# S4 and squared-ReLU gated mix, forward and gradients: an inverse FFT on half the frequencies, with mirrored frequencies in one PSUM tile and evacuations of two banks

## The chip, the cores and the metric

The kernel runs on one core of a Trainium2 chip. A core has engines that run side by side, each through its own queue in order: TensorE (PE in the profile; its weight loads are PEld), VectorE (DVE), ScalarE (ACT), GpSimd (POOL) and SyncE (SP). SP and ACT also issue the DMAs of this kernel. The metric is the time of one execution in device microseconds (us), as the median of several runs.

## The reference

The kernel computes a gated mix of two branches and all its gradients, in bfloat16, with sequence length L = 2048, width D = 448, N = 256 complex states per channel and a hidden width of F = 1792:

```python
g = sigmoid((x * gate_w).sum(-1, keepdims=True))
P = exp(dt*A * l);  K = einsum("dn,dnl,dn->dl", C, P, dt*B).real   # A, B, C complex
y = irfft(rfft(pad(u)) * rfft(pad(K)))[:L]                         # length 4096
a = y + u * Dskip
b = relu(x @ w1 + b1)**2 @ w2 + b2
out = g * a + (1 - g) * b
```

The outputs are `out` and 14 gradients (of u, the real and imaginary parts of A, B and C, log_dt, Dskip, w1, b1, w2, b2 and the gate). The gradient of the convolution needs two more transforms of the same kind: with dA the gradient that reaches the branch a, the gradient of K is the correlation of dA with u, and the gradient of u is the correlation of dA with K. So there are three forward transforms (u, dA, K) and three inverse ones (dK, y, du).

## The kernel before

**The transform.** A sequence of 2048, zero-padded to 4096, is transformed in two matrix steps over 64 × 64, with a round trip through HBM (a DRAM scratch buffer) between the two, since the second step needs the other index on the partitions. All 448 channels go side by side in the free dimension, so every matmul has 448 columns of data. The four steps are methods of `FFTCtx`:

- `fwd1` (L121–139) loads the sequence (tile `xs`), multiplies it with the constant `F1BD`, evacuates PSUM tiles `ps` to staging tiles `st` (name `st_g` here) and writes these to the scratch buffer `gd` or `gd2`.
- `fwd2` (L141–157) loads that buffer in one DMA as `s1`, multiplies with `M2` in tiles of 32 output rows, four of them side by side in the 128 PSUM partitions, and evacuates to a spectrum tile `[P, 16, 2, D]` (16 frequencies per partition group, real and imaginary part).
- `inv1` (L165–181) takes a spectrum, multiplies it with `MI`, evacuates to staging tiles (name `st_h`) and writes `hd` or `hd2` in 16 DMAs.
- `inv2` (L183–199) loads that back in 16 DMAs as tiles `hs`, multiplies with `Etw` in tiles of 32 output rows, and evacuates to a result tile (`dk_tl` or `res_tl`), which `tl_store` writes in four DMAs (L119).

The input is real, so frequency 63 − k1 of the first index holds the conjugate of frequency k1. The kernel before uses that in the forward step only (`kk = k1 if k1 < 32 else 63 - k1`): `fwd2` computes all 64 values of k1 from 32, and the inverse sums over all 64.

Each evacuation takes one bank of PSUM, 448 values per partition. `evac` (L97–103) gives two of three to ACT (L100) and the third to DVE (L102); `dma` (L93–95) alternates between the queues of SP and ACT. The PSUM pools `psF` and `psF2` hold four such tiles, the staging pools `fstg` and `fstg2` hold two of each kind, so a third staging tile waits until the DMA of the first has ended. The constants are loaded from HBM in fp32 and cast on DVE (L77–90), twice: once for each of the two places where transforms stand.

**The order of the work.** The program is one line of stages:

1. Gate and dA, parameter preparation (up to 81 us in the trace).
2. First transforms (L683–701, 81 to 284 us): `fwd1` of u and dA, `fwd2` of both (spectra `SP_U`, `SP_DA`, also stored to `sp_d`), their product `Pc` (`cmul_spec`, L586–600, on DVE), the inverse of it to `dk_tl`, and the store to `dk_d`.
3. The table stage (L706–729, to 1174 us): 17 chunks. For each, `multipliers` (L312–364) computes powers on DVE and ACT (L335 to L363), `doubling` (L366–377) builds the tables `XW` and `Yt` on DVE (L375 `U`, L376 `V`, L377 the sum), `kgen` (L398–420) makes a part of K on PE from them, and `run_chunk` (L486–571) contracts them with dK for the parameter gradients. `load_dk` (L482) brings `dk_d` back as `DK`, in two DMAs of 64 partitions each. The tables of a chunk are emitted with high priority, one chunk ahead of the contraction.
4. Transforms again (L734–842, 1174 to 1464 us): `fwd1` of K, parameter gradients (L746–827, on DVE, results `ob_…` stored by L822), `fwd2` of K (`SP_K`), then for y and du the stored spectrum is loaded (`SPx`, L833) and multiplied with `SP_K` on DVE (`PcY`, `PcU`), then `inv1` of both, `inv2` of both, and the stores to `y_d` and `du_d`.
5. The dense branch (from L844: `Un` loaded by L848, weights `w1h`, `w2h` by L894 and L896) and the final sums (L1004–1075), to 1937 us.

The order within each engine's queue is not written out by hand. The Tile framework takes the instructions in program order with their priorities and buffers and schedules them; each engine then runs its queue in order. A changed number of instructions or buffers in one stage can therefore change where instructions of the next stage stand.

Of the kernel before, what the change touches and what calls it, by code (L numbers as in the profile page):

```python
# [14 lines left out]
fp32 = mybir.dt.float32  # L15
# [4 lines left out]
P = 128  # L20
# [3 lines left out]
def host_consts():  # L24
    c = {}
    F1 = np.zeros((128, 2, 128), np.float64)
    j1 = np.arange(32)[:, None]
    k1 = np.arange(32)[None, :]
    ph = 2 * np.pi * j1 * (k1 + 0.5) / 64
    for g in range(4):  # L30
        hh, g2 = g // 2, g % 2
        F1[g * 32:(g + 1) * 32, hh, g2 * 64 + 0:g2 * 64 + 32] = np.cos(ph)
        F1[g * 32:(g + 1) * 32, hh, g2 * 64 + 32:g2 * 64 + 64] = -np.sin(ph)
    c["F1BD"] = F1.reshape(128, 256)
    M2 = np.zeros((128, 64, 2, 32), np.float64)
    j0 = np.arange(64)[:, None]
    k0 = np.arange(32)[None, :]
    for k1v in range(64):
        T = np.exp(-2j * np.pi * (j0 * (k1v + 0.5) / 4096 + j0 * k0 / 64))
        s = 1.0 if k1v < 32 else -1.0  # L40
        M2[0::2, k1v, 0, :] = T.real
        M2[1::2, k1v, 0, :] = -s * T.imag
        M2[0::2, k1v, 1, :] = T.imag
        M2[1::2, k1v, 1, :] = s * T.real
    c["M2"] = M2.reshape(128, 64 * 2 * 32)
    MI = np.zeros((128, 2, 4, 128), np.float64)
    k0 = np.arange(32)[:, None]
    l0 = np.arange(64)[None, :]
    E = np.exp(2j * np.pi * k0 * l0 / 64)
    for g in range(4):  # L50
        MI[g * 32:(g + 1) * 32, 0, g, 0:64] = E.real
        MI[g * 32:(g + 1) * 32, 0, g, 64:128] = E.imag
        MI[g * 32:(g + 1) * 32, 1, g, 0:64] = -E.imag
        MI[g * 32:(g + 1) * 32, 1, g, 64:128] = E.real
    c["MI"] = MI.reshape(128, 2 * 4 * 128)
    Et = np.zeros((128, 64, 32), np.float64)
    k1 = np.arange(64)[:, None, None]
    l0 = np.arange(64)[None, :, None]
    l1 = np.arange(32)[None, None, :]
    l = 64 * l1 + l0  # L60
    C = (2.0 / 4096) * np.exp(2j * np.pi * (k1 + 0.5) * l / 4096)
    Et[0::2] = C.real
    Et[1::2] = -C.imag
    c["Etw"] = Et.reshape(128, 64 * 32)
    return {k: v.astype(np.float32) for k, v in c.items()}


class FFTCtx:
# [52 lines left out]
    def fwd1(self, src_dram2d, gd, pool, tag="xs"):  # L121
# [19 lines left out]
    def fwd2(self, gd, sp_out, pool, tag="s1"):  # L141
        nc = self.nc
        c = self.c
# [3 lines left out]
        M2 = c["M2"]  # L147
        for k1l in range(16):
            for ro in range(2):
                ps = self.psum.tile([P, 512], fp32, tag="ps", name="ps")  # L150
                for k1g in range(4):
                    k1 = 16 * k1g + k1l
                    kk = k1 if k1 < 32 else 63 - k1
                    col = (k1 * 2 + ro) * 32
                    nc.tensor.matmul(ps[32 * k1g:32 * k1g + 32, 0:D], lhsT=M2[:, col:col + 32], rhs=s1[:, kk, :],
                                     start=True, stop=True, tile_position=(0, 32 * k1g))
                self.evac(sp_out[:, k1l, ro, :], ps[:, 0:D])

# [5 lines left out]

    def inv1(self, pspec, hd):  # L165
        nc = self.nc
        MI = self.c["MI"]
        for k1g in range(4):
            for q in range(4):
                st = self.stg.tile([P, 4, D], bf16, tag="st", name="st_h")  # L170
                for jj in range(4):
                    k1l = q * 4 + jj
                    ps = self.psum.tile([P, 512], fp32, tag="ps", name="ps")
                    for ri in range(2):
                        col = (ri * 4 + k1g) * 128
                        nc.tensor.matmul(ps[:, 0:D], lhsT=MI[:, col:col + 128], rhs=pspec(k1l, ri), start=(ri == 0), stop=(ri == 1))  # L176
                    self.evac(st[:, jj, :], ps[:, 0:D])
                k1base = 16 * k1g + q * 4
                dst = bass.AP(tensor=hd, offset=k1base * 128 * D,
                              ap=[[D, 128], [128 * D, 4], [1, D]])  # L180
                self.dma().dma_start(dst, st[:])

    def inv2(self, hd, dst_tl, ipool, tag="hs"):  # L183
        nc = self.nc
        Et = self.c["Etw"]
        for q in range(4):
            hs = ipool.tile([P, 4, 4, D], bf16, tag=tag, name=tag)
            for jj in range(4):
                src = bass.AP(tensor=hd, offset=(q * 4 + jj) * D,
                              ap=[[64 * D, 128], [16 * D, 4], [1, D]])  # L190
                self.dma().dma_start(hs[:, jj], src)
            for jj in range(4):
                l0l = q * 4 + jj
                ps = self.psum.tile([P, 512], fp32, tag="ps", name="ps")
                for l0g in range(4):
                    l0 = 16 * l0g + l0l
                    nc.tensor.matmul(ps[32 * l0g:32 * l0g + 32, 0:D], lhsT=Et[:, l0 * 32:(l0 + 1) * 32], rhs=hs[:, jj, l0g, :],
                                     start=True, stop=True, tile_position=(0, 32 * l0g))
                self.evac(dst_tl[:, l0l, :], ps[:, 0:D])

    def inv(self, pspec, hd, dst_tl):
        self.iv_i = getattr(self, "iv_i", 0) + 1
        self.inv1(pspec, hd)
        with self.tc.tile_pool(name=f"fftiv{self.iv_i}", bufs=2) as ipool:
            self.inv2(hd, dst_tl, ipool)
# [398 lines left out]
def kernel(ctx, tc, A_u, A_A_re, A_A_im, A_B_re, A_B_im, A_C_re, A_C_im, A_log_dt, A_Dskip,  # L604
# [80 lines left out]
    with tc.tile_pool(name="spB0", bufs=1) as spB0:  # L685
# [12 lines left out]
        with tc.tile_pool(name="spB1", bufs=1) as spB1:  # L698
            dk_tl = spB1.tile([P, 16, D], bf16, name="dk_tl")
            fft.inv(lambda k1l, ri: Pc[:, k1l, ri, :], hd, dk_tl)  # L700
            fft.tl_store(dk_d.ap(), dk_tl)
# [40 lines left out]
    with tc.tile_pool(name="spk", bufs=1) as spk:  # L742
# [363 lines left out]
```

## Time and profile before

| | |
|---|---|
| time, median of 3 runs | 1941.33 us (1940.83, 1941.33, 1948.38) |
| span of the profiled execution | 1936.9 us, 22440 instructions |
| busy: PE, PEld | 993.5 us (51%), 545.7 us (28%) |
| busy: DVE, ACT, POOL | 1115.7 us (58%), 974.2 us (50%), 24.3 us |
| read from HBM, written to HBM | 78.39 MB, 59.64 MB |
| mean granted TensorE clock | 0.737 |

The profiled execution has no other time of its own than its span, 1936.9 us; the median of the runs is 4.4 us above it. In the profile's rows, "L100 ACT CAST st_h<-ps" is an instruction of line 100 on ACT that writes the tile `st_h` from `ps`; an arrow with an engine or "DMA" behind an idle time names what ended the wait. A page of the profile shows the span in 40 slices of 48 us each, with one digit a slice for each engine. Rows of one stretch of time give its length, then the busy time and the number of instructions of PE, PEld, DVE, ACT and POOL, the granted clock, the DMA engines' busy share, and GB/s.

### The profile page before, as it was taken

The numbers are of one execution on the slowest core, as the hardware profiler recorded it, in microseconds if no ns is written. First come the engines' busy times: TensorE is split into PE (matmuls) and PEld (weight loads), VectorE is DVE, ScalarE is ACT, GpSimd is POOL, SyncE is SP. The second block draws the span as 40 slices with busy tenths as digits, with TensorE's granted clock in tenths as the row PEclk, the third lists the DMA queues.
The fourth block names the chain that finished last, engine by engine and source line by source line (L and its number), as shares of the span: only waits on it lengthen the run. The fifth ranks groups of instructions, "written<-read, shape, count | busy, mean of one in ns | idle before, by whom it ended". The sixth has DMA issues, their size and how long they took to land. (4 is left out here: it accounts for less than half of the span.)

```text
span 1936.9 us, 22440 instructions
## 1 busy us (share of the span) xinstructions
PE 993.5 (51%) x8145; PEld 545.7 (28%) x8160; DVE 1115.7 (58%) x1983; ACT 974.2 (50%) x1588; POOL 24.3 (1%) x77
## 2 busy tenths in 40 slices
PE   0344513345444543454445554322644999999941
PEld 0111202233223322333223331101312545544520
DVE  3426359876677777777676523687222355076347
ACT  0134348757666766677666552511432645524314
POOL 0000000000000000000000000000000000000000
PEclk9957856567667666776677765655966999999975
DMA  6575572144443234323443466532786100000032
GB/s 158 154 217 231 191 232 39 39 79 80 79 79 71 53 75 79 74 54 70 79 79 77 81 112 183 187 139 70 247 286 203 34 18 13 6 1 18 17 114 76
DMA packets 245221, 198.23 MB, mean 102 GB/s; under 512 B 25395, under 2 KB 241334, under 8 KB 242934
## 3 DMA queue, kind: packets, MB, share of 16 engines
q1 hardware_dynamic: 128566, 97.70, 20.0%
q10 hardware_dynamic: 116544, 99.10, 18.9%
q8 instruction: 64, 1.05, 0.2%
q14 instruction: 47, 0.39, 0.1%
HBM read 78.39 MB, written 59.64 MB: 71 GB/s over the span
## 5 line engine op out<-in xcount | busy, mean ns | idle before, releaser
L561 PE MATMUL psA<-Q,csb_SELA 128*128 128x256 bf16 x448 | 110.7, 324 | 191.0 <-DVE Q L557 189.4
L550 PE MATMUL psz<-yts,DKZ 128*128 128x256 bf16 x448 | 109.5, 344 | 177.4 <-ACT yts L545 143.3
L557 DVE TENSOR_TENSOR Q<-zb,XT 128x512 bf16<-128x512 bf16 x224 | 94.0, 421 | 147.0 <-ACT zb L556 88.8
L556 ACT CAST zb<-psz 128x512 bf16<-128x512 f32 x224 | 125.5, 591 | 76.5 <-PE psz L550 18.9
L506 ACT ACTIVATE DKZ<-DK,cs_MASK 128x448 bf16<-128x448 bf16 x128 | 133.7, 1104 | 7.4 <-DMA DK<-dk_d 6.6
L543 PE MATMUL ytp<-identb,Yt 128*128 128x128 bf16 x896 | 95.5, 260 | 72.1 <-ACT XTp L521 70.8
L545 ACT COPY yts<-ytp 128x1024 bf16<-128x1024 bf16 (+1 forms) x128 | 113.9, 915 | 17.2 <-issue 7.2
L563 PE MATMUL psB<-Qs,csb_SELB 128*128 128x256 bf16 x448 | 111.5, 327 | 14.7 <-DVE Qs L558 14.2
L550 PEld LDWEIGHTS <-DKZ 128*128 128x128 bf16 x448 | 52.3, 119 | 206.2 <-issue 190.8
L100 ACT CAST st_h<-ps 128x448 bf16<-128x448 f32 x127 | 61.1, 537 | 97.1 <-DMA hd<-st_h 59.7
L543 PEld LDWEIGHTS <-Yt 128*128 128x128 bf16 x896 | 78.7, 119 | 85.7 <-issue 73.4
L558 DVE TENSOR_TENSOR Qs<-zb,XTsw 128x512 bf16<-128x512 bf16 x224 | 93.4, 420 | 7.1 <-DMA XTsw<-XTp 3.8
L176 PEld LDWEIGHTS <-cb_MI 128*128 128x128 bf16 x384 | 40.9, 108 | 178.3 <-issue 130.2
L563 PEld LDWEIGHTS <-csb_SELB 128*128 128x128 bf16 x448 | 44.0, 113 | 159.6 <-issue 143.4
L102 DVE CAST st_h<-ps 128x448 bf16<-128x448 f32 x65 | 39.3, 622 | 82.3 <-DMA hd<-st_h 57.0
L375 DVE TENSOR_TENSOR U<-XW,PRX 128x224 bf16<-128x224 bf16 (+4 forms) x80 | 71.6, 895 | 19.9 <-ACT XW L391 14.8
L176 PE MATMUL ps<-PcY,cb_MI 128*128 128x448 bf16 x128 | 39.1, 455 | 82.3 <-DVE st_h L102 41.8
L519 PE MATMUL xtp<-identb,XW 128*64 128x128 bf16 x896 | 63.7, 254 | 29.6 <-DVE XW L377 28.2
L375 DVE TENSOR_TENSOR U<-Yt,PRY 128x112 bf16<-128x112 bf16 (+2 forms) x96 | 74.1, 771 | 2.4 <-POOL Yt L385 1.9
L377 DVE TENSOR_TENSOR Yt<-U,V 128x112 bf16<-128x112 bf16 (+2 forms) x96 | 74.3, 774 | 0.8
L376 DVE TENSOR_TENSOR V<-Yt,PIY 128x112 bf16<-128x112 bf16 (+2 forms) x96 | 74.0, 770 | 0.0
L377 DVE TENSOR_TENSOR XW<-U,V 128x224 bf16<-128x224 bf16 (+4 forms) x80 | 71.7, 897 | 3.1
(259 smaller groups left out, 2201.5 us busy)
## 6 DMA issues: line engine op xcount, KB each, us to landing
XT<-XTp SPq DMA_DIRECT2D x64, 224.0 KB
XTsw<-XTp ACTq DMA_DIRECT2D x128, 112.0 KB
XTsw<-XTp SPq DMA_DIRECT2D x128, 112.0 KB
XT<-XTp ACTq DMA_DIRECT2D x64, 224.0 KB
hd<-st_h ACTq DMA_DIRECT2D x24, 448.0 KB
hd<-st_h SPq DMA_DIRECT2D x24, 448.0 KB
hs<-hd ACTq DMA_DIRECT2D x24, 448.0 KB
hs<-hd SPq DMA_DIRECT2D x24, 448.0 KB
```

The costliest lines, as they stand in the source:

```text
L176: nc.tensor.matmul(ps[:, 0:D], lhsT=MI[:, col:col + 128], rhs=pspec(k1l, ri), start=(ri == 0), stop=(ri == 1))
L375: nc.vector.tensor_tensor(out=U, in0=lo, in1=PR[:, lev].unsqueeze(2).to_broadcast([P, W, n, 2]), op=ALU.mult)
L377: nc.vector.tensor_tensor(out=tab[:, :, n:2 * n, :], in0=U, in1=V, op=ALU.add)
L506: nc.scalar.activation(dst, dkv, ACT.Copy, scale=cst["MASK"][:, 2 * s + tt:2 * s + tt + 1])
L543: nc.tensor.transpose(ytp[:, qq, h * P:(h + 1) * P], src, T.identb[:])
L545: nc.scalar.copy(yts[:, 0:nq, :], ytp[:, 0:nq, :])
L550: nc.tensor.matmul(psz[:, qq, :], lhsT=DKZ[:, q0 + j].rearrange("p s a t -> p (s a t)"), rhs=yts[:, j, :], start=True, stop=True)
L556: nc.scalar.copy(zb[:], psz[:])
L557: nc.vector.tensor_tensor(out=Q[:], in0=zb[:], in1=XT[:, l0:l0 + 2, :], op=ALU.mult)
L558: nc.vector.tensor_tensor(out=Qs[:], in0=zb[:], in1=XTsw[:, l0:l0 + 2, :], op=ALU.mult)
L561: nc.tensor.matmul(psA[:], lhsT=cst["SELA"][:, 110 - 2 * dc:238 - 2 * dc], rhs=Q[:, qq, :], start=(dc == 0), stop=(dc == CC - 1))
L563: nc.tensor.matmul(psB[:], lhsT=cst["SELB"][:, 110 - 2 * dc:238 - 2 * dc], rhs=Qs[:, qq, :], start=(dc == 0), stop=(dc == CC - 1))
```

## The change

The inverse now sums only over the 32 values of k1 that are not conjugates of another, and takes twice the real part by its constants. `M2`, `MI` and `Etw` are laid out anew for that (`M2` keeps its size, `MI` shrinks from 1024 to 256 columns, `Etw` from 2048 to 1024). What this does to each step:

- `fwd2`: a PSUM tile of two banks, real and imaginary part, holds two values of kk, each with kk and its mirror 63 − kk in 64 of the 128 partitions. A matmul has 64 output rows instead of 32; there are 64 of them instead of 128, and 16 evacuations of 896 values instead of 32 of 448. The spectrum tile keeps its shape, with another meaning of its index.
- `inv1`: matmuls over 64 rows, two row tiles of the array side by side (`tile_position=(64*kk2, 0)`), 64 instead of 128; 16 evacuations of 896 values; 8 DMAs to `hd` of 448 KB instead of 16.
- `inv2`: 8 DMAs of 448 KB from `hd` instead of 16, each now to 64 partitions with runs of 2 × 448 values (before: to 128 partitions with runs of 448 values); 64 matmuls over 64 rows with 32 output rows each; 8 evacuations of 896 values instead of 16 of 448.
- `fwd1`: the same matmuls and DMAs, with evacuations of 896 values, 16 instead of 32.

All PSUM tiles of the transforms are now `[P, 2, 512]` in fp32, with the pools still at four: eight banks instead of four. The rest of the kernel is untouched; its lines stand 9 further down from `S4Tables` on (L477 is the old L468), and `evac` is L112 and L114, the write of `hd` L190, its load L199.

```diff
 # host_consts: M2, MI and Etw laid out anew, for kk = 0..31 with its mirror 63 - kk
-    M2 = np.zeros((128, 64, 2, 32), np.float64)
+    M2 = np.zeros((128, 32, 2, 2, 32), np.float64)
-    MI = np.zeros((128, 2, 4, 128), np.float64)
+    MI = np.zeros((2, 2, 32, 2, 2, 64), np.float64)
-    Et = np.zeros((128, 64, 32), np.float64)
+    Et = np.zeros((2, 32, 2, 4, 8, 32), np.float64)
...
 # fwd1
-                for jj in range(4):
-                    j0p = q * 4 + jj
-                    ps = self.psum.tile([P, 512], fp32, tag="ps", name="ps")
-                    nc.tensor.matmul(ps[:, 0:D], lhsT=F1[:, hh * 128:(hh + 1) * 128], rhs=xs[:, j0p, :], start=True, stop=True)
-                    self.evac(st[:, jj, :], ps[:, 0:D])
+                for j2 in range(2):
+                    ps = self.psum.tile([P, 2, 512], fp32, tag="ps", name="ps")
+                    for jj in range(2):
+                        j0p = q * 4 + j2 * 2 + jj
+                        nc.tensor.matmul(ps[:, jj, 0:D], lhsT=F1[:, hh * 128:(hh + 1) * 128], rhs=xs[:, j0p, :], start=True, stop=True)
+                    self.evac(st[:, 2 * j2:2 * j2 + 2, :], ps[:, :, 0:D])
...
 # fwd2
-        for k1l in range(16):
+        for i in range(16):
+            ps = self.psum.tile([P, 2, 512], fp32, tag="ps", name="ps")
             for ro in range(2):
-                ps = self.psum.tile([P, 512], fp32, tag="ps", name="ps")
-                for k1g in range(4):
-                    k1 = 16 * k1g + k1l
-                    kk = k1 if k1 < 32 else 63 - k1
-                    col = (k1 * 2 + ro) * 32
-                    nc.tensor.matmul(ps[32 * k1g:32 * k1g + 32, 0:D], lhsT=M2[:, col:col + 32], rhs=s1[:, kk, :],
-                                     start=True, stop=True, tile_position=(0, 32 * k1g))
-                self.evac(sp_out[:, k1l, ro, :], ps[:, 0:D])
+                for kk2 in range(2):
+                    kk = 2 * i + kk2
+                    nc.tensor.matmul(ps[64 * kk2:64 * kk2 + 64, ro, 0:D], lhsT=M2[:, kk, ro, :], rhs=s1[:, kk, :],
+                                     start=True, stop=True, tile_position=(0, 64 * kk2))
+            self.evac(sp_out[:, i], ps[:, :, 0:D])
...
 # inv1 (the loops over k1g and q, 16 staging tiles, become one over q with 8)
+        for q in range(8):
+            st = self.stg.tile([P, 4, D], bf16, tag="st", name="st_h")
+            for ii in range(2):
+                i = 2 * q + ii
+                pss = [self.psum.tile([P, 2, 512], fp32, tag="ps", name="ps") for _ in range(1)]
+                for ri in range(2):
+                    for kk2 in range(2):
+                        r0 = 64 * kk2
+                        nc.tensor.matmul(pss[0][:, kk2, 0:D], lhsT=MI[r0:r0 + 64, ri, :], rhs=sp[r0:r0 + 64, i, ri, :],
+                                         start=(ri == 0), stop=(ri == 1), tile_position=(r0, 0))
+                self.evac(st[:, 2 * ii:2 * ii + 2, :], pss[0][:, :, 0:D])
+            dst = bass.AP(tensor=hd, offset=4 * q * 128 * D, ap=[[D, 128], [128 * D, 4], [1, D]])
+            self.dma().dma_start(dst, st[:])
...
 # inv2
-            hs = ipool.tile([P, 4, 4, D], bf16, tag=tag, name=tag)
-            for jj in range(4):
-                src = bass.AP(tensor=hd, offset=(q * 4 + jj) * D,
-                              ap=[[64 * D, 128], [16 * D, 4], [1, D]])
-                self.dma().dma_start(hs[:, jj], src)
+            hs = ipool.tile([P, 4, 2, D], bf16, tag=tag, name=tag)
+            for hp in range(2):
+                src = bass.AP(tensor=hd, offset=(8 * hp + 2 * q) * D, ap=[[64 * D, 64], [16 * D, 4], [1, 2 * D]])
+                self.dma().dma_start(hs[64 * hp:64 * hp + 64].rearrange("p g x d -> p g (x d)"), src)
+            for x in range(2):
+                ps = self.psum.tile([P, 2, 512], fp32, tag="ps", name="ps")
                 for l0g in range(4):
+                    for hp in range(2):
+                        nc.tensor.matmul(ps[32 * l0g:32 * l0g + 32, hp, 0:D], lhsT=Et[64 * hp:64 * hp + 64, l0g, 2 * q + x, :],
+                                         rhs=hs[64 * hp:64 * hp + 64, l0g, x, :],
+                                         start=True, stop=True, tile_position=(64 * hp, 32 * l0g))
+                l0l = 2 * q + x
+                self.evac(dst_tl[:, l0l:l0l + 9:8, :], ps[:, :, 0:D])
...
-    fft2.inv1(lambda k1l, ri: PcY[:, k1l, ri, :], hd)
-    fft2.inv1(lambda k1l, ri: PcU[:, k1l, ri, :], hd2)
+    fft2.inv1(PcY, hd)
+    fft2.inv1(PcU, hd2)
```

The change also moves instructions that it does not touch, since the scheduler places them anew. On ACT, at the end of the first inverse, these rows stood before (`dk_tl` is the result, `tA` to `tD` are the temporaries of the multipliers, L337 to L344, and `cs_SELA` a selection constant):

```order
L100 CAST dk_tl<-ps 128x448 x4
L468 DMA cs_SELA<-cs_SELA 128x238
L119 DMA dk_d<-dk_tl 32x7168
L337 ACT_TABLE_LOAD
L337 ACTIVATE tC<-tA 128x616
L339 ACTIVATE tD<-tA 128x616
L341 ACT_TABLE_LOAD
L341 ACTIVATE tB<-tB 128x616
L342 ACTIVATE tD<-tD 128x616
L119 DMA dk_d<-dk_tl 32x7168
L344 ACTIVATE tD<-tD 128x616
```

In the changed kernel the same multipliers (now L346 to L353, and L362 to L372) stand near the beginning of that inverse, among its first evacuations to `st_h`:

```order
L705 DMA sp_d<-SP_DA 128x14336
L112 CAST st_h<-ps 128x896 x4
L190 DMA hd<-st_h 128x4x448
L350 ACTIVATE tB<-tB 128x616
L112 CAST st_h<-ps 128x896
L346 ACT_TABLE_LOAD
L346 ACTIVATE tC<-tA 128x616
L348 ACTIVATE tD<-tA 128x616
L190 DMA hd<-st_h 128x4x448
L351 ACTIVATE tD<-tD 128x616
L364 ACTIVATE PIY<-tC 128x336
```

So the multipliers of the first two chunks moved from behind the last evacuations, where a `dk_d` store stood among them, to a place ahead of most of the evacuations and DMAs of the inverse on ACT.

On SP, in stage 4, these rows stood before, from the last stores of the parameter gradients to the store of y (`hs` and `st_h` as above, `dlog_b` the gradient of log_dt):

```order
L822 DMA out_dram<-ob_dBr 64x256
L181 DMA hd<-st_h 128x4x448
L822 DMA out_dram<-ob_dAr 64x256
L825 DMA out_dram<-dlog_b 128x3x1
L826 DMA out_dram<-dlog_b 64x1
L181 DMA hd<-st_h 128x4x448 x7
L191 DMA hs<-hd 128x4x448 x4
L181 DMA hd<-st_h 128x4x448 x7
L191 DMA hs<-hd 128x4x448 x7
L119 DMA y_d<-res_tl 32x7168 x2
```

And these rows stand there now:

```order
L831 DMA out_dram<-ob_dBr 64x256
L190 DMA hd<-st_h 128x4x448
L831 DMA out_dram<-ob_dAr 64x256
L903 DMA w1h<-in_B_w_dram 128x896 x2
L834 DMA out_dram<-dlog_b 128x3x1
L835 DMA out_dram<-dlog_b 64x1
L905 DMA w2h<-in_B_w_dram 128x7x448
L190 DMA hd<-st_h 128x4x448 x3
L199 DMA hs<-hd 64x4x896 x2
L190 DMA hd<-st_h 128x4x448 x3
L199 DMA hs<-hd 64x4x896 x4
L131 DMA y_d<-res_tl 32x7168 x2
```

The writes and loads of the scratch buffers are half as many, and three loads of the dense branch's weights moved from behind the stores of du to a place ahead of six of the writes. From its second chunk on, the table stage has the same order as before on DVE, ACT, SP and POOL.

More of the change, by code (lines that the diff above doesn't have):

```diff
@@ L45, in host_consts @@
-    c["M2"] = M2.reshape(128, 64 * 2 * 32)
-    MI = np.zeros((128, 2, 4, 128), np.float64)
+    for kk in range(32):
+        for which in range(2):
+            k1v = kk if which == 0 else 63 - kk
+            T = np.exp(-2j * np.pi * (j0 * (k1v + 0.5) / 4096 + j0 * k0 / 64))
+            sg = 1.0 if which == 0 else -1.0
+            M2[0::2, kk, 0, which] = T.real
+            M2[1::2, kk, 0, which] = -sg * T.imag
+            M2[0::2, kk, 1, which] = T.imag
+            M2[1::2, kk, 1, which] = sg * T.real
@@ L163, in fwd, with inv1 @@
             self.fwd2(gd, sp_out, fpool)
-    def inv1(self, pspec, hd):
+    def inv1(self, sp, hd):
         nc = self.nc
[L167 to L170, printed above, removed]
-                for jj in range(4):
[L172 to L181, printed above, removed]
+        MI = self.c["MI"][:].rearrange("p (r m) -> p r m", r=2)
+        for q in range(8):
[4 more added lines that the diff above has]
+                for ri in range(2):
+                    for kk2 in range(2):
+                        r0 = 64 * kk2
[4 more added lines that the diff above has]
+            self.dma().dma_start(dst, st[:])
@@ L699 @@
             dk_tl = spB1.tile([P, 16, D], bf16, name="dk_tl")
[L700 removed]
+            fft.inv(Pc, hd, dk_tl)
             fft.tl_store(dk_d.ap(), dk_tl)
```

61 lines of the change are left out of this document (26 added, 35 removed).

## Prediction

> **What bounds the kernel now.** I read the page's span and slices first, then the busy time by stage, then who waits for whom in the stages that the change touches.
>
> ```profile
> span 1936.9 us, 22440 instructions
> ...
> DVE  3426359876677777777676523687222355076347
> ...
> DMA  6575572144443234323443466532786100000032
> ```
>
> No engine is full throughout; the stages have different limits. DMA is high at both ends of the table stage, where the transforms stand. The same by stretch (columns: length, busy time of PE, PEld, DVE, ACT, POOL, clock, DMA share, GB/s):
>
> ```profile
> 199.00:235.00 36.00, 24.21 (x111) 10.85 (x109) 12.19 (x21) 18.00 (x38) 0.00 (x0) 0.97 0.61 205
> 235.00:260.00 25.00, 7.78 (x64) 1.39 (x64) 2.66 (x5) 5.13 (x10) 0.00 (x0) 0.51 0.95 294
> ...
> 304.00:1174.00 870.00, 412.57 (x4900) 277.13 (x4899) 603.84 (x1068) 583.90 (x861) 17.16 (x56) 0.68 0.38 72
> ```
> ```profile
> 1379.00:1420.00 41.00, 27.38 (x124) 12.19 (x123) 11.80 (x20) 19.07 (x40) 0.00 (x0) 0.92 0.74 250
> 1422.00:1435.00 13.00, 4.32 (x40) 0.75 (x39) 2.16 (x4) 3.23 (x8) 0.00 (x0) 0.68 1.00 321
> ```
>
> The first row is inv1 of the first inverse, the second its inv2: no engine is busy for its length there, and the reads fill the DMA engines (0.95). The last two are the second and third inverse, alike. Their waits, from 1346 to 1464 us (total, times, longest):
>
> ```profile
> ACT st_h L100 <- DMA hd<-st_h: 50.8, 15, 26.9
> PEld L197 <- DMA hs<-hd: 39.0, 15, 7.2
> ...
> DVE st_h L102 <- DMA hd<-st_h: 34.8, 14, 6.3
> ```
> ```profile
> hd<-st_h ACTq DMA_DIRECT2D x24, 448.0 KB
> ...
> hs<-hd SPq DMA_DIRECT2D x24, 448.0 KB
> ```
>
> So the inverse is bound by its round trip through HBM: 16 writes and 16 reads of 448 KB (458,752 bytes) each. The change halves exactly these.
>
> **First inverse.** Its chain in the trace (start, length, instruction):
>
> ```profile
> 197.54 1.09 DVE L600 TENSOR_TENSOR Pc<-cm,cm 128x1792 bf16<-128x1792 bf16 x1
> 200.22 32.16 SPq L181 DMA_DIRECT2D hd<-st_h  x8
> 234.85 1.97 ACTq L191 DMA_DIRECT2D hs<-hd  x3
> 259.83 0.62 DVE L102 CAST dk_tl<-ps 128x448 bf16<-128x448 f32 x1 [2.91 <-PE ps L197]
> 264.64 0.31 ACTq L119 DMA_DIRECT2D dk_d<-dk_tl  x1
> 270.81 0.60 SPq L482 DMA_DIRECT2D DK<-dk_d  x1
> 274.12 0.35 DVE L375 TENSOR_TENSOR U<-XW,PRX 128x224 bf16<-128x224 bf16 x1 [0.36 <-ACT XW L391]
> 284.51 1.08 ACT L506 ACTIVATE DKZ<-DK,cs_MASK 128x448 bf16<-128x448 bf16 x1 [6.65 <-DMA DK<-dk_d]
> 302.49 2.02 DVE L377 TENSOR_TENSOR Yt<-U,V 128x3584 bf16<-128x3584 bf16 x1
> 304.56 1.72 PE L410 MATMUL psk<-Yt,XW 128*32 128x64 bf16 x112 [14.51 <-DVE Yt L377]
> ```
>
> *Writes.* 37.3 us pass from 197.5 to the first hs load, 16 writes in 36 us or 2.25 us each. Eight would take 18 us, but the order of ACT puts the first two chunks' multipliers between the evacuations, and an in-order queue holds the later evacuations and their DMAs behind that work. It stands behind them now:
>
> ```profile
> 261.38 1.28 ACT L337 ACT_TABLE_LOAD   x1 [0.64 <-ACT dk_tl L100]
> ...
> 272.73 0.51 ACT L363 ACTIVATE PIX<-tC 128x280 bf16<-128x280 f32 x1
> ```
>
> One chunk takes 12 us of ACT from its first table load to its last PIX. I let one of the two chunks show and the other hide behind the writes: 18 + 12 = 30, less about 1 us where ACT runs ahead, 29 us instead of 37: −8 (bounds −18 if both hide, 0 if about 20 us show).
>
> *Reads.* 25 us at 294 GB/s for 7.34 MB. Half of that is 12.5 us, plus about 1 us at the end for the larger last tile: −12.
>
> *Start of the tables.* The second dk_d store is issued 4.8 us after the last evacuation, behind a table load, and the table doubling (L375) starts 14.3 us after that evacuation. With the multipliers done early, the doubling waits only for the store to land, 270.8 − 264.6 = 6.2 us plus issue and the copies into XW, about 9 us: −5. The DK load, 13.7 us, then ends before Yt is ready, as now.
>
> *Evacuations of two banks*, which the trace does not show. The nearest rows:
>
> ```profile
> L100 ACT CAST st_h<-ps 128x448 bf16<-128x448 f32 x127 | 61.1, 537 | 97.1 <-DMA hd<-st_h 59.7 <-PE ps L176 32.3 <-DVE cm L594 4.8
> ...
> L556 ACT CAST zb<-psz 128x512 bf16<-128x512 f32 x224 | 125.5, 591 | 76.5 <-PE psz L550 18.9 <-issue 15.6 <-DVE Qs L558 14.2
> ```
> ```profile
> 146.93 6.23 ACT L100 CAST SP_U<-ps 128x448 bf16<-128x448 f32 x14 [0.15 <-PE ps L155]
> ```
>
> 64 more elements cost 54 ns, 0.84 ns each, so 896 take about 0.91 us against 1.07 for two; back to back two take 0.89 now (6.23/14 each), and 0.82 if the same overlap holds. Only fwd2 runs at that pace (16 tiles): about −2 each, and 384 KB and 512 KB less of constants to load: −3 for this stage (bounds 0 and −6). In fwd1 and inv1 the evacuations wait for buffers, so nothing.
>
> Sum here: −28. The table stage, 870 us, has the same order from its second chunk on, with its own loop; I let it start earlier and last as long: −28 at its end.
>
> **Second and third inverse.** The chain:
>
> ```profile
> 1265.13 1.09 DVE L593 TENSOR_TENSOR cm<-SPx,SP_K 128x1792 bf16<-128x1792 bf16 x1 [3.90 <-DMA out_dram<-ob_dAr]
> ...
> 1343.99 1.08 DVE L600 TENSOR_TENSOR PcU<-cm,cm 128x1792 bf16<-128x1792 bf16 x1
> 1463.20 0.57 PE L197 MATMUL ps<-hs,cb_Etw 128*32 128x448 bf16 x4 [0.21 <-DMA hs<-hd]
> 1463.81 0.40 SPq L848 DMA_DIRECT2D Un<-in_A_u_dram  x1
> ```
>
> Until 1345.1 DVE works through the products; that stays. Eight banks let PE leave s1 earlier, so the SPx load starts earlier and the 3.9 us idle go: −4. From 1345.1 to 1463.8 are 118.7 us. After: DVE still evacuates the seventh tile behind the products, so 3 of Y's 8 writes are out by then. Five writes at 2.25 are 11 us; U's eight with Y's eight reads, 7.34 MB at the mixed 250 GB/s, 29; U's reads and the y_d store (3.67 + 1.84 MB) at 321 GB/s, 17; the last tile 2: 59 us, −60. The weight loads w1h and w2h now stand in SP's and ACT's queues ahead of later hd writes and wait for the parameter stores to land; the writes behind them wait for DVE's products anyway (cost 0, or up to 5 if a store is late). Un still waits for the last reader of the constants it overlays, so the FFN follows as now.
>
> Sum: 1936.9 − 28 − 4 − 60 = 1845 us span. The median, 1941.33, is 4.4 above the profiled span; that gives **1849 us**.
>
> **PE.** Matmuls halve in number in fwd2 and inv1 and stay at 64 per inv2, now with 64 rows. For alternating column tiles the trace shows full overlap; for 64-row tiles it shows nothing:
>
> ```profile
> 147.40 5.30 PE L155 MATMUL ps<-s_u,cb_M 128*32 128x448 bf16 x72
> ...
> L176 PEld LDWEIGHTS <-cb_MI x384: 95/98/152, 176.6 to 1419.0; 128*128 128x128 bf16 x192
> ...
> L197 PE MATMUL ps<-hs,cb_Etw x192: 349/556/581, 239.1 to 1463.2; 128*32 128x448 bf16 x192
> ```
>
> 72 matmuls in 5.30 us are 74 ns each: column tiles side by side. If row tiles overlap too, an inverse has 128 matmuls of under 0.35 us, hidden under DMA. The Trainium skill (TensorEngine Tiling (Array Packing), Key Properties) says that a change of tiling mode, not of tile, drains TensorE; inv1 and inv2 each keep one mode, so by it the sum is unchanged, which the 74 ns support for columns only.
>
> **Rivals.**
>
> *Half the ports (15%).* Each hs load now fills 64 adjacent partitions. If such a load runs at half the rate, and SP's and ACT's halves do not overlap, 3.67 MB take 25 us, as 7.34 MB did: the −12 goes, and in the late stage about 12 of the reads' gain for U and 10 for Y. 1849 + 34 = 1883. For it: nothing here loads adjacent halves; against it: the two halves are issued on two queues at once, and DK's two 64-partition loads run together in 13.7 us. [...]
>
> *The table stage swallows the early start (12%).* If ACT's multipliers and evacuations hold the first inverse, or the table stage's loop re-forms later, the −28 shrinks to −5: 1872.
>
> *Writes speed up as well (10%).* If two-bank staging frees buffers sooner and Y's writes slip in under DVE's products, 15 to 25 us more: about 1828.
>
> *PE becomes the bound: slower (5%).* Row tiles that do not overlap and drain at every switch: 128 × (0.581 + 0.152) = 94 us of PE per inverse, 282 for three, where the three stages last 36 + 25 + 118.7 = 180 now. Less some 15 us under the products, that is 1941 + 87 = 2028. It decides from 180/384 = 0.47 us per matmul. Against it: column tiles show no such cost.
>
> *Nothing moves (3%).* DMA is not cut as claimed, or later waits eat it all: within 10 us of 1941. 0.5%, 10 us, is about what a measurement of this kernel can tell from no change.
>
> **Numbers.** The forecast has 55%. Its own bounds (−18 to 0 on writes, 0 to −6, up to +5) give 1832 to 1864; reaching to the ports case and to the faster one, 1824 to 1885 leaves out the slow and the unmoved cases and a little more. Faster 0.92, same 0.03, slower 0.05.
>
> **What the changed profile would show.** Right: 8 hd writes and 8 hs loads per inverse; the first hs load about 29 us after the last Pc product; inv2 at about 13 us with a DMA share over 0.9; the doubling about 28 us earlier; from the last PcU to the Un load about 59 us; an ACT cast of 896 at about 0.91 us; the table stage at 870 us. Wrong: a DMA share near 0.5 in inv2 (ports), PE busy through inv1 and inv2 (row tiles), or a table stage that is longer by what was won ahead of it.

## The result, and the profile after

The changed kernel takes 1864.49 us (median of 4 runs, 1863.84 to 1866.95) where the kernel before took 1943.24 us (median of 4 runs, 1940.83 to 1948.38): a ratio of 0.9606, with a 95% interval from 0.9579 to 0.9634. The forecast was faster, at 1849 us within 1824 to 1885; it named the right way and held the time in its range, and it was about 15 us too low. The profiled execution has a span of 1863.0 us, 73.9 us under that of before, where 92 us were forecast.

The page of the changed kernel, to set beside the rows of before:

```profile
span 1863.0 us, 21223 instructions
...
DMA  6576471234443343244234456733982100000032
...
HBM read 65.54 MB, written 48.63 MB: 61 GB/s over the span
```

The bytes fell as claimed, by 12.85 MB read (78.39 before) and 11.01 MB written (59.64 before): three times 3.67 MB each way for the inverses, and the smaller constants. The table stage still stands between the two pieces of transforms, at the same DMA share.

The stretches that the prediction spoke of, in the changed kernel (columns as before: length, PE, PEld, DVE, ACT, POOL, clock, DMA share, GB/s):

```profile
198.00:221.00 23.00, 5.89 (x28) 2.04 (x27) 11.69 (x17) 22.11 (x33) 0.00 (x0) 0.50 0.36 120
221.09:242.37 21.28, 4.87 (x64) 0.82 (x64) 3.27 (x3) 4.43 (x5) 0.00 (x0) 0.50 0.83 173
1315.00:1336.00 21.00, 7.58 (x36) 2.70 (x36) 3.56 (x4) 5.24 (x6) 0.00 (x0) 0.50 0.80 142
1336.00:1358.00 22.00, 10.39 (x72) 3.35 (x71) 6.46 (x6) 9.81 (x12) 0.00 (x0) 0.50 0.78 220
1358.00:1390.30 32.30, 9.66 (x96) 1.62 (x96) 4.37 (x4) 6.42 (x8) 0.00 (x0) 0.50 0.94 235
```

Read the second row against its counterpart of before, 25 us at 294 GB/s and a share of 0.95. Half the bytes now take 21.3 us: the DMA engines are still busy for 0.83 of the stretch, but move 173 GB/s. The reads were made half as many and the rate fell by 40%. The first row shows another thing: ACT is busy for 22.11 of 23 us, and the DMA share is 0.36, so the writes of the first inverse are no longer bound by DMA.

The timeline of the changed kernel shows the first inverse from its last product to the start of the tables:

```profile
196.89 1.09 DVE L609 TENSOR_TENSOR Pc<-cm,cm 128x1792 bf16<-128x1792 bf16 x1
...
221.09 1.25 ACTq L199 DMA_DIRECT2D hs<-hd  x2
...
226.30 0.53 PE L204 MATMUL ps<-hs,cb_Etw 64*32 64x448 bf16 x1 [12.83 <-DMA hs<-hd]
228.30 0.95 PE L204 MATMUL ps<-hs,cb_Etw 64*32 64x448 bf16 x15 [1.47 <-DMA hs<-hd]
...
236.47 0.95 PE L204 MATMUL ps<-hs,cb_Etw 64*32 64x448 bf16 x16 [3.74 <-DMA hs<-hd]
...
241.46 0.91 ACT L112 CAST dk_tl<-ps 128x896 bf16<-128x896 f32 x1 [2.62 <-PE ps L204]
242.39 1.15 ACTq L131 DMA_DIRECT2D dk_d<-dk_tl  x2
...
251.67 0.45 ACT L399 CAST XW<-PG_cWr 128x56 bf16<-128x56 f32 x1 [9.31 <-DMA dk_d<-dk_tl]
...
253.80 0.36 DVE L384 TENSOR_TENSOR U<-XW,PRX 128x224 bf16<-128x224 bf16 x1 [6.54 <-POOL XW L396]
```

PE waits for each tile of hs again (1.47 and 3.74 us here), and takes 0.95 us for all 16 matmuls of a tile, where one alone takes 0.53: the row tiles and the column tiles run side by side. The same in the late inverses, from the last product to the load of Un:

```profile
1313.86 1.08 DVE L609 TENSOR_TENSOR PcU<-cm,cm 128x1792 bf16<-128x1792 bf16 x1
1313.98 0.38 ACTq L190 DMA_DIRECT2D hd<-st_h  x1
...
1325.59 1.71 ACT L112 CAST st_h<-ps 128x896 bf16<-128x896 f32 x2 [20.81 <-DMA hd<-st_h]
...
1336.18 1.22 SPq L199 DMA_DIRECT2D hs<-hd  x2
...
1369.05 0.80 SPq L131 DMA_DIRECT2D y_d<-res_tl  x2
...
1390.34 0.40 SPq L857 DMA_DIRECT2D Un<-in_A_u_dram  x1
```

The write that ACT issues at 1314.0 has landed when ACT goes on at 1325.6: 11.6 us for 448 KB. The same write in the kernel before:

```profile
1344.10 0.38 ACTq L181 DMA_DIRECT2D hd<-st_h  x1
...
1351.25 1.40 ACT L100 CAST st_h<-ps 128x448 bf16<-128x448 f32 x3 [26.95 <-DMA hd<-st_h]
```

It let ACT go on after 7.15 us.

### The profile page after: what moved, and what is told of

It reads as the page before. It is cut to its first block, busy times and chain, and to the rows that moved or that the text cites. A ratio compares the mean times of both kernels' runs of the same rounds, so it can differ in the third digit from the quotient of the medians.

```text
span 1863.0 us, 21223 instructions
## 1 busy us (share of the span) xinstructions
PE 920.8 (49%) x7761; PEld 517.4 (28%) x7776; DVE 1088.2 (58%) x1895; ACT 932.1 (50%) x1412; POOL 24.2 (1%) x77
## 5 line engine op out<-in xcount | busy, mean ns | idle before, releaser
L565 ACT CAST zb<-psz 128x512 bf16<-128x512 f32 x224 | 125.7, 592 | 74.2 <-PE psz L559 17.8
L572 PE MATMUL psB<-Qs,csb_SELB 128*128 128x256 bf16 x448 | 110.9, 325 | 13.6 <-DVE Qs L567 13.4
L528 PE MATMUL xtp<-identb,XW 128*64 128x128 bf16 x896 | 63.8, 254 | 27.3 <-DVE XW L386 25.9
L385 DVE TENSOR_TENSOR V<-XW,PIX 128x224 bf16<-128x224 bf16 (+4 forms) x80 | 71.1, 888 | 0.0
L570 PEld LDWEIGHTS <-csb_SELA 128*128 128x128 bf16 x448 | 45.0, 111 | 91.2 <-issue 74.3
L530 ACT COPY XTp<-xtp 128x1024 bf16<-128x1024 bf16 x64 | 66.2, 1044 | 0.5 <-PE xtp L528 0.5
L367 ACT CAST PRX<-tA 128x280 bf16<-128x280 f32 x32 | 15.9, 496 | 97.9 <-DVE U L384 81.9
```

The lines of the kernel that those rows point to most:

```text
L385: nc.vector.tensor_tensor(out=V, in0=rev_last(lo), in1=PI[:, lev].unsqueeze(2).to_broadcast([P, W, n, 2]), op=ALU.mult)
L565: nc.scalar.copy(zb[:], psz[:])
L570: nc.tensor.matmul(psA[:], lhsT=cst["SELA"][:, 110 - 2 * dc:238 - 2 * dc], rhs=Q[:, qq, :], start=(dc == 0), stop=(dc == CC - 1))
L572: nc.tensor.matmul(psB[:], lhsT=cst["SELB"][:, 110 - 2 * dc:238 - 2 * dc], rhs=Qs[:, qq, :], start=(dc == 0), stop=(dc == CC - 1))
```

## The experiments

All of them start from the changed kernel unless they say so, and ratios are to the kernel before on the same chip. The table has the stages in each profiled execution, in us, by the starts and ends of the rows shown above.

| kernel | last Pc end to first hs | inv2 of the first inverse | its end to U | U to load of K | gd to SPx | last PcU end to first hs | first hs to Un | ratio |
|---|---|---|---|---|---|---|---|---|
| before | 36.2 | 25.9 | 13.4 | 902.6 | 56.9 | 34.7 | 84.0 | 1 |
| changed | 23.1 | 21.3 | 11.4 | 899.0 | 49.3 | 21.2 | 54.2 | 0.9606 |
| changed, second profile | 23.1 | 21.2 | 12.9 | 902.8 | 49.5 | 20.1 | 54.7 | 0.9604 |
| evacuations only | 32.6 | 26.2 | 12.9 | 902.9 | 49.7 | 33.1 | 83.9 | 0.9915 |
| half spectrum only | 31.2 | 21.4 | 12.3 | 902.7 | 53.3 | 19.9 | 59.5 | 0.9719 |
| 128 partitions per load | 23.1 | 17.6 | 12.0 | 899.3 | 51.7 | 21.9 | 48.7 | 0.9590 |
| runs of 896 B | 23.1 | 21.7 | 12.2 | 900.6 | 49.3 | 18.6 | 53.2 | 0.9613 |
| four hs buffers | 15.3 | 19.7 | 13.5 | 904.1 | 49.8 | 18.8 | 54.4 | 0.9572 |
| 128 partitions, four hs buffers | 15.3 | 14.8 | 13.1 | 904.6 | 53.7 | 17.9 | 48.2 | 0.9518 |
| inverse ahead of multipliers | 6.8 | 21.5 | 12.5 | 915.3 | 49.1 | 19.7 | 54.0 | 0.9597 |
| weights late | 23.1 | 21.2 | 12.0 | 901.0 | 48.9 | 17.8 | 54.7 | 0.9583 |
| three staging buffers | 22.5 | 21.3 | 11.2 | 900.4 | 46.0 | 20.3 | 50.1 | 0.9546 |
| 128 partitions, four hs buffers, weights late | 15.3 | 14.6 | 13.3 | 901.7 | 53.7 | 16.6 | 47.6 | 0.9518 |
| the same, three staging buffers | 11.6 | 14.8 | 13.1 | 905.6 | 52.1 | 15.0 | 43.2 | 0.9431 |

The dense branch behind Un, which no kernel touches but for its weights' loads, took between 467 and 474 us in these profiles. Differences of a few us in the whole time are therefore no evidence; the stages are.

### The changed kernel once more

> The changed kernel as it is, beside the others on the same chip: about 0.9606 of before, and the stages within 2 us of those of its first profile up to the dense branch.

Ratio 0.9604 (0.9585 to 0.9623). Up to U its stages agree within 2 us. Its table stage took 902.8 us, as before the change, against 899.0 in the first profile: 3.8 us between two executions of the same program.

### Which half of the change

Evacuations of two banks in the kernel before, with its full spectrum:

```diff
 # kernel before, inv1; likewise in fwd1, fwd2 and inv2
-                for jj in range(4):
-                    ps = self.psum.tile([P, 512], fp32, tag="ps", name="ps")
+                for j2 in range(2):
+                    ps = self.psum.tile([P, 2, 512], fp32, tag="ps", name="ps")
...
-                    self.evac(st[:, jj, :], ps[:, 0:D])
+                    self.evac(st[:, 2 * j2:2 * j2 + 2, :], ps[:, :, 0:D])
```

> The full spectrum of the kernel before (16 writes and 16 reads of 448 KB per inverse), with evacuations of two banks in all four steps and eight banks of PSUM. Theory: the gain of the change comes from the halved round trip, and the evacuations only shorten the forward steps; the forward step of K, from its first gd write to the SPx load, goes from 56.9 to about 50 us, the rest stays, and the time falls by 3 to 12 us against the kernel before (about 1934). Rival: two-bank evacuations and eight banks carry most of the gain; then it falls by 35 us or more (under 1908).

Ratio 0.9915 (0.9897 to 0.9933), 1921.48 us beside 1938.16: 16.7 us, more than the theory's 12 and half of what the rival asked for. The forward step of K fell from 56.9 to 49.7 us as expected; 3.6 us more came from the writes of the first inverse and 4.9 from what lies ahead of its last product.

The counterpart, the half spectrum with one bank per evacuation:

```diff
-            ps = self.psum.tile([P, 2, 512], fp32, tag="ps", name="ps")
             for ro in range(2):
+                ps = self.psum.tile([P, 512], fp32, tag="ps", name="ps")
...
-            self.evac(sp_out[:, i], ps[:, :, 0:D])
+                self.evac(sp_out[:, i, ro], ps[:, 0:D])
```

> The half spectrum of the changed kernel, with evacuations of one bank and four banks, as before. Theory: the halved round trip carries the gain, so 1864 plus the forward steps' part of 7 to 10 us: about 1873. Rival (evacuations carry it): over 1900.

Ratio 0.9719 (0.9699 to 0.9739). The two parts, 0.85% and 2.81%, make 3.66% of the 3.94% together: within the intervals they add, and the bytes carry most of it. Against the changed kernel about 22 us are missing (0.9719 − 0.9606, of 1938), not the 7 to 10 expected: 8.1 of them in the writes of the first inverse (31.2 against 23.1), where ACT is the bound; 5.3 lie behind the first late hs load and 4.0 in the forward step of K.

### Why the reads did not get twice as fast

Each load of the changed kernel fills partitions 0–63 or 64–127. This variant interleaves the rows of the two halves, so that a load covers all 128 partitions, with the same size, count and runs; `Etw` is doubled, with zeros for the other half's rows, and the matmuls have 128 rows again. The two loads of a tile read the same stretches of `hd` in both kernels, only dealt out differently, so what is read from HBM does not differ.

```diff
-            for hp in range(2):
-                src = bass.AP(tensor=hd, offset=(8 * hp + 2 * q) * D, ap=[[64 * D, 64], [16 * D, 4], [1, 2 * D]])
-                self.dma().dma_start(hs[64 * hp:64 * hp + 64].rearrange("p g x d -> p g (x d)"), src)
+            for gh in range(2):
+                src = bass.AP(tensor=hd, offset=(16 * gh + 2 * q) * D, ap=[[32 * D, 128], [8 * D, 2], [1, 2 * D]])
+                self.dma().dma_start(hs[:, 2 * gh:2 * gh + 2].rearrange("p g x d -> p g (x d)"), src)
...
```

> The changed kernel, where each hs load covers all 128 partitions (rows of the two halves interleaved, two of the four l0g groups per load) instead of 64 adjacent ones; still 448 KB per load in runs of 1792 B, 8 loads, the same writes; Etw is twice as large, with zeros. Theory (partitions): loads of 64 adjacent partitions run at a lower rate; with 128 the first inverse's inv2 goes from 21 us (221.1 to 242) to about 13.5, and the late reads of y and du lose about 10 us more: about 1847. Rival 1 (longer runs are slower) and rival 2 (four loads in flight instead of eight are too few): inv2 stays at 20 to 22 us and the time at 1862 to 1867.

Its inv2, as one stretch:

```profile
223.27:240.87 17.60, 6.77 (x64) 2.01 (x64) 3.28 (x3) 4.43 (x5) 0.00 (x0) 0.50 0.62 209
```

17.6 us: 3.7 less than the changed kernel, and not the 13.5 of the theory. The DMA share, though, fell from 0.83 to 0.62 while the rate rose from 173 to 209 GB/s. With loads of 64 adjacent partitions the DMA engines are kept busy by a transfer that moves slowly; with 128 they have time left, so something else holds the loads back. The whole time, 1858.55 us, is not the 1847 of the theory, and its ratio overlaps with that of the changed kernel; from the first late hs load to Un 5.5 us are gone (48.7 against 54.2), not about 10.

The length of the runs is not it:

```diff
-                src = bass.AP(tensor=hd, offset=(8 * hp + 2 * q) * D, ap=[[64 * D, 64], [16 * D, 4], [1, 2 * D]])
-                self.dma().dma_start(hs[64 * hp:64 * hp + 64].rearrange("p g x d -> p g (x d)"), src)
+                src = bass.AP(tensor=hd, offset=(8 * hp + q) * D, ap=[[64 * D, 64], [16 * D, 4], [4 * D, 2], [1, D]])
+                self.dma().dma_start(hs[64 * hp:64 * hp + 64], src)
...
```

> The changed kernel, with hs loads of 64 adjacent partitions as it has them, but in runs of 896 B (positions q and q + 4 instead of 2q and 2q + 1). Theory now (partitions and loads in flight set the rate): inv2 of the first inverse stays at 21 to 22 us, the time at 0.960 to 0.963 of before. Rival (long runs are slow): 18 us or less.

```profile
219.44:241.14 21.70, 4.86 (x64) 0.82 (x64) 3.27 (x3) 4.43 (x5) 0.00 (x0) 0.50 0.83 169
```

The same 21.7 us, the same share and the same rate with twice as many runs of half the length.

A tile of hs held four loads before and holds two now, so two buffers let four loads of 448 KB be in flight where there were eight. With four buffers:

```diff
-            hs = ipool.tile([P, 4, 2, D], bf16, tag=tag, name=tag)
+            hs = ipool.tile([P, 4, 2, D], bf16, tag=tag, name=tag, bufs=4)
...
-        with self.tc.tile_pool(name=f"fftiv{self.iv_i}", bufs=2) as ipool:
+        with self.tc.tile_pool(name=f"fftiv{self.iv_i}", bufs=4) as ipool:
```

> The changed kernel with four hs buffers instead of two, so that all eight loads of an inverse can be in flight, as eight of sixteen were before; still 64 adjacent partitions per load. If too few loads in flight are the rest of the loss: inv2 falls from 21.3 to 17 or 18 us, as it did with loads of 128 partitions. If the partitions alone count: it stays at 20 to 22.

```profile
212.95:232.62 19.67, 5.41 (x64) 0.92 (x64) 3.46 (x4) 4.43 (x5) 0.00 (x0) 0.50 0.82 187
```

Only 1.6 us, and the DMA share stays at 0.82. Seven of the eight loads are in flight at once here (issued by 215.4); ACT issues the eighth behind two evacuations, at 224.4. It lands 2.0 us after the seventh, where the others follow each other by 1.3 to 2.2 us, so little is lost by that. Both together:

> Loads of 128 partitions and four hs buffers together. If both count and add: inv2 falls from 21.3 to 13 or 14 us (half of the 24.4 before, plus the last tile), and the time to about 0.950 of before (about 15 us under the changed kernel, half of it in the late reads). If only one of them counts: 17 to 18 us, and 0.957.

```profile
214.47:229.28 14.81, 6.78 (x64) 2.02 (x64) 3.84 (x5) 4.43 (x5) 0.00 (x0) 0.50 0.71 248
```

14.8 us at 248 GB/s. The four cases form a square: 21.3 with neither, 17.6 with 128 partitions, 19.7 with four buffers, 14.8 with both. Each counts without the other, the partitions for 3.7 or 4.9 us and the buffers for 1.6 or 2.8, and together they come within 1.3 us of the 13.5 that were forecast. The whole time falls to a ratio of 0.9518 (0.9496 to 0.9541). These two kernels with four buffers also have the multipliers elsewhere on ACT (15.3 us in the first column instead of 23.1), which comes from the scheduler and not from the reads; behind U they take 904 us, where the changed kernel took 899 and 902.8. The second of them also has the dense branch's weights later (shown below), so its whole time is not that of the loads alone.

The rows tell the two causes apart. Length times DMA share times 16 engines, divided by the 2048 runs of 1792 B of an inverse's loads, is the time for which one run keeps an engine busy: about 138 ns in the changed kernel and 126 with four buffers, 85 and 82 with loads of 128 partitions. So the partitions set how long a run takes. With 128 partitions the buffers leave that time nearly as it is and fill idle time of the DMA engines: the share rises from 0.62 to 0.71.

### The multipliers ahead of the writes

```diff
-            fft.inv(Pc, hd, dk_tl)
-            fft.tl_store(dk_d.ap(), dk_tl)
+            with tc.high_priority():
+                fft.inv(Pc, hd, dk_tl)
+                fft.tl_store(dk_d.ap(), dk_tl)
...
-                with tc.high_priority():
+                with (tc.high_priority() if c > 0 else ExitStack()):
```

> The changed kernel, with the first inverse scheduled ahead of the first chunk's multipliers, so that ACT evacuates st_h without them in between. Theory: the DMA gap of about 8 us at 201 to 208.6 comes from ACT, in order; the first hs load comes 8 to 10 us earlier (about 212), the multipliers hide under the reads, and the doubling (L384 U) starts 6 to 9 us earlier: 1856 to 1859. Rival: the multipliers then stand between the store and the doubling, and it starts when it does now: 1862 to 1867.

The first hs load came 16.3 us sooner behind the last product (6.8 instead of 23.1), more than the 8 to 10 expected, and U started at 239.7 instead of 253.8. The multipliers did hold the writes. But the load of K came at 1155.0, no sooner than in the changed kernel (1152.8): all 14 us were given back inside the table stage, by a wait that neither theory had. The timeline of this kernel:

```profile
237.26 0.63 ACTq L491 DMA_DIRECT2D DK<-dk_d  x1
...
242.57 0.63 DVE L384 TENSOR_TENSOR U<-XW,PRX 128x896 bf16<-128x896 bf16 x1
...
251.15 1.05 ACT L515 ACTIVATE DKZ<-DK,cs_MASK 128x448 bf16<-128x448 bf16 x1 [12.15 <-DMA DK<-dk_d]
252.22 1.28 ACT L346 ACT_TABLE_LOAD   x1
253.51 0.72 ACT L346 ACTIVATE tC<-tA 128x616 f32<-128x616 f32 x1
254.26 0.80 DVE L357 TENSOR_TENSOR tC<-tB,tC 128x616 f32<-128x616 f32 x1 [10.54 <-ACT tC L346]
255.63 1.09 DVE L384 TENSOR_TENSOR U<-XW,PRX 128x1792 bf16<-128x1792 bf16 x1
```

ACT waits 12.15 us for the DK load with the second chunk's multipliers behind it in its queue; DVE has the first product that needs these multipliers (L357) in the middle of the doubling, and waits 10.54 us there. By the end of the first Yt the lead was gone (281.0 here, 281.6 in the changed kernel). The whole time is at 0.9597 (0.9581 to 0.9614), not to be told from the changed kernel.

### The weights ahead of the writes

```diff
+        if fh == 0:
+            nc.gpsimd.tensor_copy(w1h[:, 0:3, 0], Un[:, 0:3, 0])
...
+            nc.gpsimd.tensor_copy(w2h[:, 0, 0:1], Un[:, 0, 0:1])
```

> The changed kernel, where the first half of the weights w1h and w2h is loaded only after Un (a small copy from Un into them on POOL goes first). Theory: these loads, now just ahead of the writes of PcY, slow the first ACT write from 7 to 11.6 us; without them the first late hs load comes 4 to 5 us nearer to the last PcU (21.2 to about 17), and Un's issue is 4 to 5 us earlier; the dense branch starts with w1h still loading, so of that 0 to 5 us reach the end: 1857 to 1862 on the scale of 1864. Rival: the writes are held by their own rate, nothing moves, or the dense branch waits for the weights and the time rises by up to 5 us.

```profile
1315.43 0.37 ACTq L190 DMA_DIRECT2D hd<-st_h  x1
...
1323.45 1.71 ACT L112 CAST st_h<-ps 128x896 bf16<-128x896 f32 x2 [26.78 <-DMA hd<-st_h]
```

The first write of ACT lands after 8.0 us instead of 11.6, and the first hs load comes 17.8 us behind the last product instead of 21.2 (20.1 in the second profile of the changed kernel). In all profiles with the weights ahead of it this write takes 8.8 to 12.5 us to land, and in those with the weights behind it, the kernel before among them, 6.9 to 8.0: the loads do slow it. The first hs load follows less clearly, since with the weights ahead its column spans 18.6 to 21.9. The ratio, 0.9583 (0.9567 to 0.9599), overlaps with that of the changed kernel, so how much of it reaches the end stays open.

### Staging buffers, and all together

Three staging buffers instead of two:

```diff
-            st = self.stg.tile([P, 4, D], bf16, tag="st", name="st_h")
+            st = self.stg.tile([P, 4, D], bf16, tag="st", name="st_h", bufs=3)
...
-                st = self.stg.tile([P, 4, D], bf16, tag="st", name="st_g")
+                st = self.stg.tile([P, 4, D], bf16, tag="st", name="st_g", bufs=3)
```

> The changed kernel with three staging buffers for st_g and st_h instead of two. If the writes of the late inverses are held by the buffers (ACT waits 36.5 us for writes of hd to end there): from the last PcU to Un's issue 3 to 8 us less than 75.4, and fwd1 of K shorter by some us. If they are held by the rate of the DMAs: 75 us again, within 2.

From the last PcU to Un 70.4 us against 75.4 (74.8 in the second profile), from gd to SPx 46.0 against 49.3, and the ratio 0.9546 (0.9526 to 0.9565), 11 us under the changed kernel beside it: the buffers hold a part of the writes. In the late inverses that part lies behind the first hs load (50.1 us against 54.2), not in the writes of y (20.3 us against 21.2 and 20.1). The loads of 128 partitions, four hs buffers and late weights together, by the three diffs above:

> Loads of 128 partitions, four hs buffers and the late weights together. If the three causes are separate: the loads' 17 us and the weights' 3 to 4 add up, about 0.950 of before; from the last PcU to Un's issue about 62 us (66.1 with the loads alone, less 3 to 4). If the weights only mattered beside slow loads: 0.952, as with the loads alone.

Ratio 0.9518 (0.9498 to 0.9538), the same as the kernel with 128 partitions and four buffers, and 64.2 us from the last PcU to Un where 62 were expected and that kernel had 66.1. This pair cannot price the weights, because in that kernel the scheduler had already placed their first half behind Un:

```profile
1375.13 0.37 SPq L857 DMA_DIRECT2D Un<-in_A_u_dram  x1
...
1392.14 0.83 SPq L903 DMA_DIRECT2D w1h<-in_B_w_dram  x2
```

In the changed kernel their issue begins at 1302.9 us, 87 us ahead of Un. With three staging buffers on top:

> The same with three staging buffers: if buffers hold the writes, 3 to 8 us under the run without them (0.947); if the DMA rate does, the same within 2 us.

Ratio 0.9431 (0.9414 to 0.9448), 1831.89 us beside 1940.89 of before and 1864.43 of the changed kernel on the same chip. It is the fastest of all, and 17 us under the same without the third buffer, where 3 to 8 were expected.

## Why the prediction was right, and where its sizes were off

**The bound** was the round trip through HBM, and halving it carried most of the gain: 2.81% of 3.94% with the half spectrum alone, and the bytes fell as claimed.

**Writes of the first inverse**, −8: −13 came, by two errors that partly cancel. From the start of the last product to the first hs load 24.2 us passed instead of the forecast 29. The mechanism is the one named, ACT's multipliers between the evacuations; with the inverse scheduled ahead of them 7.9 us are left from the same start. So the multipliers cost about 16 us, more than the 12 that I let show, and the writes alone 8 us instead of 18. I had put all eight writes behind the last product, where all sixteen stand before the change; the changed kernel issues two ahead of that product's end (at 181.2 and 195.1 of 198.0 us), and the kernel with the inverse ahead six. That the sum came near is luck.

**Reads of the first inverse**, −12: this step failed in its size. It took the rate of before, 294 GB/s, for half the bytes, and the rate fell to 173: 21.3 us instead of 13.5, −4.6 and not −12. It had no term for the loads in flight, four instead of eight. The rival of half the ports had the right place. The runs show that the rate falls with loads of 64 adjacent partitions even when both halves are issued at once on two queues, and that fewer bytes in flight take most of the rest. The Trainium skill (SBUF — State Buffer, Door 1: The DMA port swizzle) has partitions 0–63 reach one half of the 16 ports and 64–127 the other. The trace agrees in the direction, 21.3 against 17.6 us and a DMA share of 0.83 against 0.62, and shows that two such loads on two queues don't make up for it. That it is the ports, and not something else about 64 adjacent partitions, is argued and not shown. I gave this rival a loss of the whole −12; the partitions alone cost 3.7 to 4.9 us of it.

Against this rival I had set the two loads of `DK`, of 64 partitions each. They do not bear on it: `DK2[t:P:2]` gives each of them every second one of the 128 partitions. From 270.8 to 284.5 us in the kernel before, they move 3.67 MB, in runs of 896 B and 1792 KB a load, at 268 GB/s with a DMA share of 0.88. So a load of 64 partitions need not be slow; the slow ones have them side by side.

**Start of the tables**, −5: it was −2 (−0.5 in the second profile). The doubling did wait for the store alone, but 9.3 us passed from the last evacuation until the whole store had landed, where I had taken 6.2 from the issue of its last part.

**Evacuations of two banks**, −3 in this stage: the duration was right (904 ns on ACT against the forecast 0.91 us):

```profile
L112 ACT CAST st_h<-ps 128x896 bf16<-128x896 f32 x32 | 27.9, 904 | 66.6 <-DMA hd<-st_h 45.2 <-PE ps L186 10.6 <-DVE cm L603 10.2
```

At the last product the changed kernel was only 0.7 us ahead in one profile and 1.4 behind in the other, while the evacuations alone were 4.9 ahead. In fwd1 I had counted nothing; from the first gd write to the SPx load the transform of K became 7.6 us shorter, 7.2 of which the evacuations alone give.

**The table stage** lasted as long as before, as forecast: 899.0 and 902.8 us against 902.6 from U to the load of K. The sum to there was −24.0 in the first profile and −16.8 in the second, instead of −28; 3.6 of the −24.0 are the table stage's own difference, no more than lies between the two profiles.

**Second and third inverse.** Up to the last PcU −6 came instead of −4. Behind it, 118.7 us became 75.4 and not 59: −43 instead of −60. Of the 16 missing us, 10 lie in the writes of y (21.2 us where 11 were forecast) and the other 6 between the first hs load and Un. For the writes, I had put the weight loads at 0 to 5; between profiles they cost 0.8 to 4. Without them 17.8 us still stand against the 11, and a third staging buffer alone leaves 20.3, so the larger part of this miss stays open. For the rest, the forecast took 250 and 321 GB/s, and the rows of the changed kernel show 220 and 235. With loads of 128 partitions its 48 us from the first hs load to Un come about, 48.7 with two hs buffers and 48.2 with four, against 54.2 in the changed kernel. That the match is so close is partly luck, since a third staging buffer brings this stretch down to 43.2.

**PE** never became the bound. A tile's 16 matmuls of 64 rows take 0.95 us, where one alone takes 0.53, so at 60 ns each they run side by side. In the kernel with loads of 128 partitions the matmuls have 128 rows, so that only column tiles stand side by side, and the same 16 take 1.69 us:

```profile
228.17 1.69 PE L204 MATMUL ps<-hs,cb_Etw 128*32 128x448 bf16 x16 [12.54 <-DMA hs<-hd]
```

The row tiles do overlap, and the rival that had them in a row falls.

**The bounds.** The forecast's own bounds, 1832 to 1864, do not quite come out of their terms: 1849 less 10 on the writes and 3 on the evacuations is 1836, and with 8, 3 and 5 added it is 1865. The stated range, 1824 to 1885, follows from the times of the rivals instead.

## What to carry to other kernels

Halving the bytes of a transfer halves its time only if the new transfers keep the rate of the old, so look at what each load covers (here 128 partitions became 64) and how many of them the buffers let fly, before you divide by two. A high DMA share says that the engines are occupied, not that they move bytes at their usual rate; read it together with the GB/s (here 0.83 at 173 GB/s against 0.62 at 209). An early start is worth something only up to the next wait: with in-order queues, a wait for a load that stands ahead of unrelated work can give all of it back.

## What the runs showed that was not expected

Four loads of 448 KB in flight, over 128 partitions, moved 209 GB/s, and eight 248; with 64 adjacent partitions it was 173 with four and 187 with seven. Runs of 896 B and of 1792 B made no difference (169 and 173 GB/s). A third staging buffer, which the change did not touch, was worth 11 us on the changed kernel and 17 us on the one with better loads, with whatever the scheduler moved beside it.
